# An attention stage whose scores, row transposes, sign bits and sums move into one ring of PSUM bank pairs, with a new order of the work

## The chip, the cores and the metric

The kernel runs on one core of a Trainium2 chip. The metric is the device time of one execution in microseconds (us). TensorE is called PE, VectorE DVE, ScalarE ACT, GpSimd POOL, and SyncE, which issues all the DMAs, SP. PSUM, the memory that PE writes its results to, has eight banks of 512 float32 values in each of 128 partitions.

## The reference

Attention with a hash mask, then two MLP stages on its output; about 18% of the time before is attention, and only attention is changed.

```python
q_bits = (q @ proj > 0)                  # 6 sign bits per query, the same for k
mask   = bucket(q_bits)[:, None] == bucket(k_bits)[None, :]
scores = where(mask, (q @ k.T) / 8, -1e9)
attn   = exp(scores - scores.max(-1))
attn   = attn / (attn.sum(-1) + 1e-9)
x      = attn @ v                        # 2 x 8 heads, 768 tokens, 64 per head
x      = moe(x); out = moe2(x)
```

## The kernel before

There are 16 heads. The queries of a head are worked on in two halves of 384, which makes 32 units; the code calls a unit `u`. Two units (one half of two neighbouring heads) make a pair `n`, and there are 16 pairs. For each unit:

- `s_mm(u, t)`, three times: PE multiplies 128 queries by all 768 keys into the PSUM tile `ps` (lines 376 to 380, two matmuls of together 768 columns), and `s_max(u, t)` reduces it on DVE to the negated maximum of each query (line 383). The mask is part of the product: 12 rows that hold the sign bits stand under the 64 rows of the head.
- `rows_mm(u)` transposes the three columns of maxima on PE (line 392; for the first four units line 390), `rows_cp(u)` copies them on DVE (line 403), and from unit 4 on `rows_move(u)` sends them by DMA into row 96 of the queries' operand.
- `st_mm(u, c)`, six times: the transposed scores of 128 keys, with the row of maxima added, by two matmuls of 384 columns into `pst` (lines 411 and 412); `st_exp(u, c)` takes their exponential on ACT (line 417). `pst` has two banks, so the third `st_mm` waits for the first exponential, and so on.
- `add` sums the exponentials of a unit on POOL (line 429). For a pair, `sum_mm(n)` sums these over the partitions into `psum` (line 455), and `av_mm(n, g)`, twice, multiplies the exponentials by v into `pav` (line 439, twelve matmul passes). `norm` divides, in seven parts on DVE, ACT and POOL with four DMAs (`norm_move`).
- `bits_mm(h)` and `bits_cmp(h)` make the sign bits of a later head (lines 350 and 353); `prep_hi`, `prep_lo`, six `prep_move` and four `bits_move` per head bring operands into place, the moves as DMAs on SP.

Beside this, eight half blocks of weights of the next stage are decoded (`decode`, `weight_hi`, `weight_lo`).

The PSUM of attention before: one tile `s_all` of 1536 values, three banks, holds two score tiles of 768 next to each other, so that the middle bank holds the end of the first and the start of the second. `t_all` is two banks for `pst`; from unit 4 on the row transposes lie in the unused last 128 columns of these. Two banks are `pav`, and the eighth, `ps_m`, is used in turn by the sign bits, the sums and the first units' rows.

The order of the work is made by a planner when the kernel is built: every task has engines, a cost, a due time and the tasks it comes after. Each step takes the task whose planned start plus DELTA times its due time is least. OFF holds a number for each kind of task that is added to its due time. AVD is an offset in the due time of `av_mm`, DUE0 and PACE set the due times of the weight decode. A task with `ring="m"` waits in the plan until the ring's last user is freed. On the chip each engine runs its own list in order, with semaphores between engines.

Of the kernel before, what the change touches and what calls it, by code (L numbers as in the profile page):

```python
# [16 lines left out]
P = 128  # L17
# [5 lines left out]
E = 8  # L23
# [14 lines left out]
NS = 4  # L38
# [4 lines left out]
AVD = 9  # L43
# [7 lines left out]
OFF = {'norm5': 36.2, 'bits_move': 7.5, 'norm1': 2.8, 'bits_mm': 1.0, 'load_v': 17.1, 'norm3': 0.4, 'norm_move': -5.2, 'norm7': 18.8, 'norm0': 8.2, 'weight_load': 32.5, 'weight_lo': 7.6, 'prep_hi': 4.6, 'av_one': -0.2, 'prep_lo': 3.5, 'decode': -2.5, 'norm6': 3.8, 'weight_hi': 23.9, 'rows_mm': 2.9, 'av_mm': -0.5, 'load_qk': -6.3, 'norm4': 13.6, 'rows_cp': -3.6, 'prep_move': 2.8, 'sum_mm': -8.7, 's_max': 2.5, 'rows_move': -4.1, 'bits_cmp': 0.7, 'st_exp': -4.0, 'add': 0.0, 'st_mm': -0.1, 's_mm': -0.3}  # L51
DELTA = 0.0206
RECEIPT = 1.6
DIRECT = 4
DUE0 = 60
PACE = 25
# [15 lines left out]
def lsh_attention_moe_kernel(  # L72
# [111 lines left out]
    def attention():  # L184
        with ExitStack() as a:
# [37 lines left out]
            s_all = ps_s.tile([P, 2 * S], F32, name="ps")  # L223
            t_all = [ps_t.tile([P, 512], F32, name=f"pst{i}") for i in range(2)]
# [60 lines left out]
            def warm_up():  # L285
                warm.append(t_all[0])
                for _ in range(WARM):
                    nc.tensor.matmul(warm[0], xh[:, 0, 0:P], xh[:, 0, 0:512], start=True, stop=True)

            def keep_warm(n):  # L290
                if nm(av_one, 1, 0) in ends:
                    return
                if nm(st_mm, 0, 0) in ends and len(warm) == 1:
                    if nm(av_one, 0, 0) in ends:
                        return
                    warm.append(slot(ps_a, "a", 1, 2, [P, 512], F32, "warm"))
                for _ in range(n):
                    nc.tensor.matmul(warm[-1][:, :FILL], xh[:, 0, 0:P], xh[:, 0, 0:FILL], start=True, stop=True)
# [73 lines left out]
            def s_of(u, t):  # L372
                x = (3 * u + t) % 2
                return s_all[:, x * S:(x + 1) * S]

            def s_mm(u, t):
                s, q0, x = head(u) % NS, half_of(u) * HALF + t * P, (3 * u + t) % 2
                cuts = sorted({0, (512, 256)[x], S} | ({HALF} if u == 0 else set()))
                for a, b in zip(cuts, cuts[1:]):
                    nc.tensor.matmul(s_of(u, t)[:, a:b], sq[s][0:96, q0:q0 + P], bk[s][0:96, a:b], start=True, stop=True)  # L380

            def s_max(u, t):
                nc.vector.tensor_reduce(out=mx_t[u % 2][:, t:t + 1], in_=s_of(u, t), axis=AX.X, op=ALU.max, negate=True)  # L383
# [107 lines left out]
            def task(engines, due, f, *args, after=(), cost=None, lag=0.01, ring=None, frees=None):  # L491
# [14 lines left out]
                    clear=0.6, prep_lo=1.0, add=1.08, norm=1.0, decode=1.3, weight_lo=1.27,  # L506
# [4 lines left out]
            SEEN = {"E": 0.2, "A": 0.05, "D": 0.05, "P": 0.06}  # L511
# [28 lines left out]
            for h in range(NH):  # L540
# [14 lines left out]
                for i in range(2):  # L555
                    task("PD" if h else "D", due - 14.0 + 1 if h else -50, prep_lo, h, i, after=[his[i if h == 0 else 0], *moved] + [los[0]] * i)
                task("E", due - 10.0 if h else -50, bits_mm, h, cost=None if h else 1.1, after=[nm(load_qk, h), nm(proj_parts)], ring="m",
                     frees=nm(bits_cmp, h) if h else nm(bits_cmp, 0, 1, 0))
# [17 lines left out]
            for u in range(NU):  # L576
                h, half, n = head(u), half_of(u), pair_of(u)
                due = 6 * u - 16.0
                for t in range(3):
                    before = nm(s_max, u, 0) if t == 2 else nm(s_max, u - 1, 1 + t)  # L580
                    task("E", due + 2 * t, s_mm, u, t,
                         after=[nm(prep_move, h, 0), nm(prep_move, h, 1), *([nm(bits_move, h, x) for x in range(4)] if h else [nm(bits_cmp, 0, *x) for x in ((0, 1), (1, 1), (half, 0))])] + ([before] if u or t == 2 else []))
                    task("D", due + 2 * t + 0.5, s_max, u, t, after=[nm(s_mm, u, t)] + [nm(rows_mm, u - 2)] * (t == 0 and u > 1))
                direct = u < DIRECT
                task("E", due + 5.5, rows_mm, u, cost=0.14 if direct else None, after=[nm(s_max, u, t) for t in range(3)] + [nm(load_const, 2)] + [nm(warm_up)] * (u == 0), ring="m" if 0 < u < DIRECT else None, frees=nm(rows_cp, u))
# [17 lines left out]
            for n in range(NU // 2):  # L603
# [3 lines left out]
                room = [nm(norm, n - 2, 5)] if n > 1 else []  # L607
# [6 lines left out]
                task("E", due + 8, sum_mm, n, after=[nm(add, u, g, 1) for u in us for g in range(2)], ring="m", frees=nm(norm, n, 0))  # L614
# [716 lines left out]
```

## Time and profile before

| | us |
|---|---|
| three runs | 1551.10, 1552.38, 1553.12 (median 1552.38) |
| the profiled execution | 1549.82 |
| its span, first to last instruction | 1547.90 |
| first instruction to the last matmul of attention | 278.5 |
| PE busy over the span | 1505.7 (97%) |

The profiled execution is 0.17% below the median of the runs; it took 1.92 us more than its span. In the profile a matmul's row gives its start and a duration that runs on while the next one starts, since matmuls are pipelined: what one costs PE's stream is the distance to the next start. "[0.34 <-DVE mx L383]" behind a row means that the engine stood idle for 0.34 us and that DVE's instruction of line 383 ended that. "x2" counts instructions that are shown in one row.

### The profile page before, as it was taken

The page shows a single profiled execution, that of the slowest core. Times are in us where ns is not written, and L with a number is a line of the kernel's source. Part 1 is how long each engine was busy: PE and PEld are TensorE (multiplying, and loading weights), DVE is VectorE, ACT ScalarE, POOL GpSimd, SP SyncE. Part 2 cuts the span into 40 slices and gives each one's busy share as a digit, 9 for nine tenths or more (in the row PEclk, how much of TensorE's full clock was granted, in tenths as well). Part 3 has the DMA queues.
Part 4 walks back from the last instruction along what each step waited for, and adds up shares of the span by engine and source line. Part 5 has one row for each costly group of instructions (what it writes and reads, how often), then busy time and mean ns, then how long its engine had stood idle before and what let it go on. Part 6 is the DMA issues. An engine that isn't in the chain of part 4 may idle for free.

```text
span 1547.9 us, 20241 instructions
## 1 busy us (share of the span) xinstructions
PE 1505.7 (97%) x7454; PEld 1256.1 (81%) x7454; DVE 861.9 (56%) x1400; ACT 628.7 (41%) x1113; POOL 902.1 (58%) x750
## 2 busy tenths in 40 slices
PE   8888888999999999999999999999999999999998
PEld 5454444688888789898989898989898999999997
DVE  6666666777752666666443467654535344445353
ACT  4444444555432443334333333343333333333331
POOL 5556666543332476666666666667666666666661
PEclk9999999999999999999999999999999999999999
DMA  7356451222110012222222221213222222221211
GB/s 185 113 123 149 109 129 42 82 83 82 64 59 1 28 56 81 69 68 69 68 67 70 67 68 66 69 60 116 64 70 66 69 68 68 68 69 68 69 55 41
DMA packets 69561, 116.80 MB, mean 75 GB/s; under 512 B 21348, under 2 KB 23512, under 8 KB 69464
## 3 DMA queue, kind: packets, MB, share of 16 engines
q1 hardware_dynamic: 69464, 115.53, 24.8%
q8 instruction: 58, 0.95, 0.3%
q14 instruction: 39, 0.32, 0.1%
HBM read 93.41 MB, written 3.15 MB: 62 GB/s over the span
## 4 chain that ended last, share of the span: by engine, by line
PE 91%; DVE 5%; DMA 1%; ACT 1%; issue 1%; SPq 1%; DVEq 0%; ACTq 0%
PE y L1183 34%; PE u L1116 30%; PE y L819 8%; PE pav L439 4%; DVE mx L383 4%; PE ps L380 3%; PE h L796 3%; PE h L794 3%; PE h L795 3%; PE pst L411 1%; PE psum L455 1%; PE pst L412 1%; DMA other<-own 1%; ACT p L417 0%; PE lg L847 0%
## 5 line engine op out<-in xcount | busy, mean ns | idle before, releaser
L1124 ACT ACTIVATE gh<-c 128x384 fp32r<-128x384 f32 x256 | 134.6, 526 | 174.3 <-DVE c L1136 172.3
L1129 DVE SCALAR_TENSOR_TENSOR gl<-c,gh 128x384 fp32r<-128x384 f32 x256 | 195.6, 826 | 0.0
L1136 DVE TENSOR_TENSOR u<-u,p 128x384 f32<-128x384 f32 x64 | 35.7, 558 | 284.2 <-PE u L1116 282.4
L1183 PE MATMUL y<-ww,gh 128*128 128x512 f32 x768 | 186.6, 391 | 0.0
L1183 PE MATMUL y<-w,gh 128*128 128x512 f32 x768 | 186.0, 391 | 0.0
L1183 PEld LDWEIGHTS y<-w,gh 128*128 128x128 f32 x768 | 143.7, 188 | 28.9
L1183 PEld LDWEIGHTS y<-ww,gh 128*128 128x128 f32 x768 | 143.7, 188 | 28.8
L417 ACT ACTIVATE p<-pst 128x384 f32<-128x384 f32 x192 | 86.0, 489 | 118.5 <-PE pst L412 77.0
L999 POOL TENSOR_TENSOR w<-stage,w 128x1024 fp32r<-128x1024 f32 x32 | 76.6, 2393 | 89.1 <-ACT w L995 89.1
L999 POOL TENSOR_TENSOR ww<-stage,ww 128x1024 fp32r<-128x1024 f32 x32 | 76.5, 2391 | 81.6 <-ACT ww L995 81.6
L383 DVE TENSOR_REDUCE mx<-ps 128x1 f32<-128x768 f32 x96 | 90.6, 953 | 47.2 <-PE ps L380 46.9
L819 PE MATMUL y<-gh,w 128*128 128x512 f32 x336 | 109.8, 389 | 0.0
L158 POOL TENSOR_TENSOR stage<-stage,sgn 128x512 f32<-128x512 f32 x32 | 43.3, 1354 | 104.7 <-DVE sgn L156 90.4
L429 POOL TENSOR_TENSOR pa<-p,p 128x384 f32<-128x384 f32 x64 | 66.1, 1033 | 61.6 <-ACT p L417 61.6
L1183 PE MATMUL y<-ww,gl 128*128 128x512 f32 x384 | 98.2, 389 | 0.0
L1183 PE MATMUL y<-w,gl 128*128 128x512 f32 x384 | 97.6, 389 | 0.0
L995 ACT CAST ww<-stage 128x1024 fp32r<-128x1024 f32 x32 | 33.6, 1050 | 157.5 <-PE y L1183 157.5
L975 POOL TENSOR_TENSOR wa<-stage,wa 128x512 fp32r<-128x512 f32 x32 | 45.5, 1421 | 88.8 <-ACT wa L970 79.7
L995 ACT CAST w<-stage 128x1024 fp32r<-128x1024 f32 x32 | 33.6, 1049 | 154.5 <-PE y L1183 154.5
L975 POOL TENSOR_TENSOR wx<-stage,wx 128x512 fp32r<-128x512 f32 x32 | 45.4, 1419 | 80.4 <-ACT wx L970 80.4
L1116 PE MATMUL u<-tw,w 128*128 128x384 f32 x480 | 91.8, 336 | 0.0
L1116 PE MATMUL u<-tw,ws 128*128 128x384 f32 x480 | 91.6, 336 | 0.0
(204 smaller groups left out, 3634.3 us busy)
## 6 DMA issues: line engine op xcount, KB each, us to landing
stage<-in_w_dram SPq DMA_DIRECT2D x160, 512.0 KB
raw<-in_qk_dram SPq DMA_DIRECT2D x13, 384.0 KB
sb<-hi SPq DMA_DIRECT2D x20, 192.0 KB
vt<-in_v_dram SPq DMA_DIRECT2D x16, 192.0 KB
out_dram<-acc SPq DMA_DIRECT2D x11, 256.0 KB
wx<-hi SPq DMA_DIRECT2D x14, 192.0 KB
zq<-hi SPq DMA_DIRECT2D x10, 192.0 KB
ak<-hi SPq DMA_DIRECT2D x10, 192.0 KB
```

The lines of the kernel that those rows point to most:

```text
L383: nc.vector.tensor_reduce(out=mx_t[u % 2][:, t:t + 1], in_=s_of(u, t), axis=AX.X, op=ALU.max, negate=True)
L417: nc.scalar.activation(p_t[u, c][:, :HALF], st_t.pop((u, c))[:, :HALF], AF.Exp, scale=0.125)
L429: (nc.gpsimd if e == "P" else nc.vector).tensor_add(t, (t if x else p_t[u, 3 * g])[:, :HALF], p_t[u, 3 * g + 1 + x][:, :HALF])
L439: nc.tensor.matmul(av_t[n][64 * e:64 * e + 64, :WIDE], vt[head(u) // 2 % 2][:, c, e, :], p_t[u, c][:, :WIDE], start=(c == 0), stop=(c == N ...
L819: nc.tensor.matmul(yps[j], x, y, start=(head and m == 0), stop=(tail and m == 2))
L975: nc.gpsimd.tensor_sub(a[:, 1, 0:512], t[:, 0, :], f32(a)[:, 0, 0:512])
L995: nc.scalar.copy(wbuf[u % 2]["w"][:, 0, :], staged["u", u, 1].rearrange("p c n -> p (c n)"))
L999: nc.gpsimd.tensor_sub(y[:, 1, :], t, f32(y)[:, 0, :])
L1116: nc.tensor.matmul(bank[x], weight(u, a, m, kc), moving(u, b, mm, kc), start=(first and n == 0), stop=(n == 5), skip_group_check=not first)
L1124: nc.scalar.activation(hi, src, AF.Relu)
L1129: nc.vector.scalar_tensor_tensor(out=lo, in0=src, scalar=0.0, in1=f32(hid_u[u, c][0]), op0=ALU.max, op1=ALU.subtract)
L1183: nc.tensor.matmul(y_t[t], (hi, hi, lo)[m][:, t % 3 * P:(t % 3 + 1) * P], y, start=(k == 0 and first), stop=(k == NF // 2 - 1 and last),)
```

## The change

Score tiles, row transposes, sign bits and sums are now all taken from one ring, `next_r`, of two slots; a slot is two whole banks, [128, 2, 512]. A score tile uses 384 columns of each of its two banks, by two matmuls of 384 columns. `s_all` and `ps_m` are gone; the four banks of the ring take their place. `pst` keeps its two banks but no longer holds row transposes. In the plan a task of ring "r" waits for the last but one user to be freed. Head 0's bits are made in a bank of `pav`. The constants of the planner are new: all 31 numbers of OFF (`st_mm` from -0.1 to 2.1, `s_mm` from -0.3 to 2.4, `sum_mm` from -8.7 to -0.6, ...), DELTA, AVD, DUE0, PACE and two costs. No arithmetic is changed.

```diff
-AVD = 9
+AVD = 6
...
-DELTA = 0.0206
+DELTA = 0.0524
...
-DUE0 = 60
-PACE = 25
+DUE0 = 20
+PACE = 24
...
-            ps_s = a.enter_context(tc.tile_pool(name="ps_s", bufs=1, space=bass.MemoryType.PSUM))
+            ps_r = a.enter_context(tc.tile_pool(name="ps_r", bufs=1, space=bass.MemoryType.PSUM))
...
-            ps_m = a.enter_context(tc.tile_pool(name="ps_m", bufs=1, space=bass.MemoryType.PSUM))
...
-            s_all = ps_s.tile([P, 2 * S], F32, name="ps")
-            t_all = [ps_t.tile([P, 512], F32, name=f"pst{i}") for i in range(2)]
+            used_r = [0]
...
-            def next_m(name):
-                return slot(ps_m, "m", 0, 1, [P, 512], F32, name)
+            def next_r(name):
+                used_r[0] += 1
+                return slot(ps_r, "r", used_r[0], 2, [P, 2, 512], F32, name)
...
-                psb_t[h] = next_m("pbits")
+                psb_t[h] = next_r("pbits")[:, 0] if h else slot(ps_a, "a", 1, 2, [P, 512], F32, "pbits")
...
-            def s_of(u, t):
-                x = (3 * u + t) % 2
-                return s_all[:, x * S:(x + 1) * S]
-
             def s_mm(u, t):
-                s, q0, x = head(u) % NS, half_of(u) * HALF + t * P, (3 * u + t) % 2
-                cuts = sorted({0, (512, 256)[x], S} | ({HALF} if u == 0 else set()))
-                for a, b in zip(cuts, cuts[1:]):
-                    nc.tensor.matmul(s_of(u, t)[:, a:b], sq[s][0:96, q0:q0 + P], bk[s][0:96, a:b], start=True, stop=True)
+                s, q0 = head(u) % NS, half_of(u) * HALF + t * P
+                s_t[u, t] = next_r("ps")
+                for j in range(2):
+                    nc.tensor.matmul(
+                        s_t[u, t][:, j, :HALF], sq[s][0:96, q0:q0 + P], bk[s][0:96, j * HALF:(j + 1) * HALF], start=True, stop=True
+                    )
...
-                m = t_all[u % 2][:, HALF:] if u >= DIRECT else next_m("prow") if u else t_all[1]
+                m = next_r("prow")[:, 0]
...
-                t = t_all[c % 2]
+                t = slot(ps_t, "t", NKC * u + c, 2, [P, 512], F32, "pst")
...
-                sum_t[n] = next_m("psum")
+                sum_t[n] = next_r("psum")[:, 0]
...
-            SEEN = {"E": 0.2, "A": 0.05, "D": 0.05, "P": 0.06}
+            SEEN = {"E": 0.28, "A": 0.05, "D": 0.05, "P": 0.06}
...
                     use = ring_use.setdefault(t[7], [])
-                    if use:
-                        if use[-1] not in ends:
+                    if len(use) >= 2:
+                        if use[-2] not in ends:
                             return None
-                        r = max(r, ends[use[-1]])
+                        r = max(r, ends[use[-2]])
```

What the new plan does to PE's list is seen in the middle of attention, around one pair's sums. Before, all that is not a score or an `st_mm` stands in one block: a row transpose, the first `av_mm`, the sums, another row transpose, and then the second `av_mm` and a later head's sign bits:

```order
L392 MATMUL pst_160<-idt,mx_157 3x128
L439 MATMUL pav<-p_144,vt_128 64x386
L439 MATMUL pav<-p_136,vt_128 64x386
L439 MATMUL pav<-p_145,vt_128 64x386
L439 MATMUL pav<-p_137,vt_128 64x386
L439 MATMUL pav<-p_146,vt_128 64x386
L439 MATMUL pav<-p_138,vt_128 64x386
L455 MATMUL psum<-pa_150,ones 32x384
L455 MATMUL psum<-pa_151,ones 32x384
L455 MATMUL psum<-pa_152,ones 32x384
L455 MATMUL psum<-pa_153,ones 32x384
L392 MATMUL pst_159<-idt,mx_156 3x128
```

In the changed kernel the six `st_mm` of one unit, with two to four score tiles, stand between the two `av_mm` of a pair. The list around the sums (line numbers are three to seven lower there):

```order
L452 MATMUL psum<-pa_147,ones 32x384
L452 MATMUL psum<-pa_148,ones 32x384
L452 MATMUL psum<-pa_149,ones 32x384
L452 MATMUL psum<-pa_150,ones 32x384
L347 MATMUL pbits<-raw,pf 32x192 x4
L436 MATMUL pav<-p_138,vt_125 64x386
L436 MATMUL pav<-p_144,vt_125 64x386
L436 MATMUL pav<-p_139,vt_125 64x386
L436 MATMUL pav<-p_145,vt_125 64x386
L436 MATMUL pav<-p_140,vt_125 64x386
L436 MATMUL pav<-p_146,vt_125 64x386
L389 MATMUL prow<-idt,mx_153 3x128
```

One `av_mm` with the sums and the bits is a block, the other `av_mm` with a row transpose another, and before and behind each stand `st_mm` and scores.

The second place is where PE writes scores. Before, two neighbouring score tiles are written into the one tile `ps_158` (names with their numbers here):

```order
L380 MATMUL ps_158<-sb1_118 128x256
L380 MATMUL ps_158<-sb1_118 128x512
L411 MATMUL pst0_159<-zq3_123,ak3_126 128x384
L412 MATMUL pst0_159<-sb3_120 128x384
L380 MATMUL ps_158<-sb1_118 128x512
L380 MATMUL ps_158<-sb1_118 128x256
```

and in the changed kernel every user of the ring is a tile of its own, here a row transpose and two score tiles:

```order
L389 MATMUL prow_1344<-idt_69,mx1_154 3x128
L408 MATMUL pst_1346<-zq2_119,ak2_122 128x384
L409 MATMUL pst_1346<-sb2_116 128x384
L373 MATMUL ps_1354<-wx0_78 128x384 x2
L408 MATMUL pst_1360<-zq2_119,ak2_122 128x384
L409 MATMUL pst_1360<-sb2_116 128x384
L373 MATMUL ps_1365<-wx0_78 128x384 x2
```

The third place is DVE's list behind a pair's sums in the changed kernel: each row that reads `ps`, `psum`, `pbits` or `prow` frees a slot of the ring, and other work stands among them.

```order
L378 TENSOR_REDUCE mx0_153<-ps_1533 128x1
L465 STREAM_TRANSPOSE rs_127<-psum_1549 128x384
L350 TENSOR_SCALAR bit_1569<-pbits_1556,cst_71 128x192
L156 TENSOR_SCALAR sgn1_87<-stage_794 128x512
L420 TENSOR_TENSOR xl_75<-xu_126,xh_74 128x384
L400 TENSOR_SCALAR row_1584<-prow_1577 3x128
L378 TENSOR_REDUCE mx1_154<-ps_1586 128x1
```

Before, `psum`, `pbits` and `prow` are not in the scores' banks, so that of these rows only the two reductions free what the scores wait for.

## Rows read from the trace of the kernel before

**Rows 1.** Windows: us, then busy (instructions) of PE, PEld, DVE, ACT, POOL; PEclk, DMA share, GB/s.
```profile
156.50:188.10 31.60, 27.72 (x158) 15.39 (x160) 20.91 (x34) 13.59 (x30) 20.50 (x20) 1.00 0.48 118
251.70:278.50 26.80, 25.27 (x143) 12.14 (x142) 16.68 (x30) 13.77 (x30) 18.64 (x18) 1.00 0.07 21
300.00:340.00 40.00, 40.00 (x178) 33.10 (x178) 31.65 (x43) 25.37 (x42) 17.02 (x10) 1.00 0.28 90
```

**Rows 2.** Timeline, PE and DVE, 120 to 124 us: start, us, engine, instruction, [idle before].
```profile
120.46 0.61 PE L380 MATMUL ps<-sb 96*128 96x256 f32 x2 [0.36 <-DVE mx L383]
121.11 0.96 DVE L383 TENSOR_REDUCE mx<-ps 128x1 f32<-128x768 f32 x1 [0.37 <-PE ps L380]
...
122.12 0.62 PE L380 MATMUL ps<-sb 96*128 96x512 f32 x2 [0.34 <-DVE mx L383]
122.78 0.96 DVE L383 TENSOR_REDUCE mx<-ps 128x1 f32<-128x768 f32 x1 [0.23 <-PE ps L380]
```

**Rows 3.** Timeline, PE and then DVE, 96 to 99 us.
```profile
96.27 0.51 PE L380 MATMUL ps<-sb 96*128 96x512 f32 x2
96.62 0.34 PE L411 MATMUL pst<-zq,ak 128*128 128x384 f32 x1
96.80 0.34 PE L412 MATMUL pst<-sb 97*128 97x384 f32 x1
...
98.69 0.61 PE L380 MATMUL ps<-sb 96*128 96x256 f32 x2 [1.01 <-DVE mx L383]
...
96.82 1.82 DVE L383 TENSOR_REDUCE mx<-ps 128x1 f32<-128x768 f32 x2 [0.73 <-PE ps L380]
```

**Rows 4.** Timeline, PE, one block of av, sums, rows and bits.
```profile
124.25 0.27 PE L392 MATMUL pst<-idt,mx 128*3 128x128 f32 x1
124.45 2.17 PE L439 MATMUL pav<-p,vt 128*64 128x386 f32 x12
126.54 0.85 PE L455 MATMUL psum<-pa,ones 128*32 128x384 f32 x8
127.33 0.27 PE L392 MATMUL pst<-idt,mx 128*3 128x128 f32 x1
127.53 2.17 PE L439 MATMUL pav<-p,vt 128*64 128x386 f32 x12
129.62 0.53 PE L350 MATMUL pbits<-raw,pf 128*32 128x192 f32 x8
130.09 0.45 PE L411 MATMUL pst<-zq,ak 128*128 128x384 f32 x1
```

**Rows 5.** Timeline, PE, where no scores are left.
```profile
270.25 0.44 PE L411 MATMUL pst<-zq,ak 128*128 128x384 f32 x1 [0.27 <-ACT p L417]
...
271.52 0.44 PE L411 MATMUL pst<-zq,ak 128*128 128x384 f32 x1 [0.26 <-ACT p L417]
```

**Rows 6.** Timeline, SP: the first of each kind of DMA issue, 156 to 174 us.
```profile
156.83 0.72 SPq L332 DMA_DIRECT2D sb<-row  x1
157.60 1.61 SPq L332 DMA_DIRECT2D sb<-bit  x2
160.41 2.48 SPq L459 DMA_DIRECT2D other<-own  x4
...
163.88 1.15 SPq L332 DMA_DIRECT2D sb<-hi  x2
...
165.84 0.47 SPq L259 DMA_DIRECT2D raw<-in_qk_dram  x1
...
173.91 1.31 SPq L265 DMA_DIRECT2D vt<-in_v_dram  x2
```

**Rows 7.** Timeline, ACT, start of attention.
```profile
24.48 0.87 ACT L417 ACTIVATE p<-pst 128x384 f32<-128x384 f32 x2 [0.33 <-PE pst L412]
34.85 0.87 ACT L417 ACTIVATE p<-pst 128x384 f32<-128x384 f32 x2 [9.50 <-PE pst L412]
```

**Rows 8.** Windows, columns as in rows 1: the stretch with a lower clock.
```profile
104.00:108.00 4.00, 3.87 (x13) 2.46 (x15) 2.33 (x5) 1.21 (x3) 1.01 (x1) 0.54 0.28 60
```

More of the change, by code (lines that the diff above doesn't have):

```diff
@@ L50 @@
 AHEAD = (1, 2)
-OFF = {'norm5': 36.2, 'bits_move': 7.5, 'norm1': 2.8, 'bits_mm': 1.0, 'load_v': 17.1, 'norm3': 0.4, 'norm_move': -5.2, 'norm7': 18.8, 'norm0': 8.2, 'weight_load': 32.5, 'weight_lo': 7.6, 'prep_hi': 4.6, 'av_one': -0.2, 'prep_lo': 3.5, 'decode': -2.5, 'norm6': 3.8, 'weight_hi': 23.9, 'rows_mm': 2.9, 'av_mm': -0.5, 'load_qk': -6.3, 'norm4': 13.6, 'rows_cp': -3.6, 'prep_move': 2.8, 'sum_mm': -8.7, 's_max': 2.5, 'rows_move': -4.1, 'bits_cmp': 0.7, 'st_exp': -4.0, 'add': 0.0, 'st_mm': -0.1, 's_mm': -0.3}
-DELTA = 0.0206
+OFF = {'weight_lo': 16.9, 'add': -3.4, 'weight_load': -20.3, 'norm6': 66.2, 'prep_hi': -4.2, 'norm_move': -19.9, 'load_qk': 0.9, 'norm0': -16.1, 'load_v': -23.6, 'decode': 9.4, 'bits_mm': -6.9, 'norm1': -61.2, 'norm5': 11.9, 'st_exp': -7.0, 'norm7': 23.6, 'rows_cp': -10.6, 'av_mm': 0.7, 'rows_move': -20.0, 'rows_mm': 3.0, 'norm4': -35.4, 'norm3': 9.3, 'sum_mm': -0.6, 'bits_cmp': -14.6, 'av_one': 3.6, 'weight_hi': 63.6, 's_max': 0.0, 'st_mm': 2.1, 'prep_move': 6.5, 'prep_lo': -0.4, 'bits_move': -5.8, 's_mm': 2.4}
+DELTA = 0.0524
 RECEIPT = 1.6
 DIRECT = 4
-DUE0 = 60
-PACE = 25
+DUE0 = 20
+PACE = 24
 NX = 1
@@ L285, in warm_up @@
             def warm_up():
-                warm.append(t_all[0])
+                warm.append(slot(ps_t, "t", 0, 2, [P, 512], F32, "warm"))
                 for _ in range(WARM):
@@ L290, in keep_warm @@
             def keep_warm(n):
-                if nm(av_one, 1, 0) in ends:
+                if nm(av_one, 0, 0) in ends:
                     return
                 if nm(st_mm, 0, 0) in ends and len(warm) == 1:
-                    if nm(av_one, 0, 0) in ends:
-                        return
-                    warm.append(slot(ps_a, "a", 1, 2, [P, 512], F32, "warm"))
+                    warm.append(slot(ps_a, "a", 0, 2, [P, 512], F32, "warm"))
                 for _ in range(n):
@@ L505, in attention @@
                 "P": dict(
-                    clear=0.6, prep_lo=1.0, add=1.08, norm=1.0, decode=1.3, weight_lo=1.27,
+                    clear=0.6, prep_lo=1.0, add=1.03, norm=1.0, decode=1.3, weight_lo=1.27,
                 ),
@@ L556, in attention @@
                     task("PD" if h else "D", due - 14.0 + 1 if h else -50, prep_lo, h, i, after=[his[i if h == 0 else 0], *moved] + [los[0]] * i)
-                task("E", due - 10.0 if h else -50, bits_mm, h, cost=None if h else 1.1, after=[nm(load_qk, h), nm(proj_parts)], ring="m",
-                     frees=nm(bits_cmp, h) if h else nm(bits_cmp, 0, 1, 0))
+                task("E", due - 10.0 if h else -50, bits_mm, h, cost=None if h else 1.1, after=[nm(load_qk, h), nm(proj_parts)] + [nm(bits_move, h - 2, x) for x in range(4) if h > 2], ring="r" if h else None, frees=nm(bits_cmp, h))
                 if h:
@@ L579, in attention @@
                 for t in range(3):
-                    before = nm(s_max, u, 0) if t == 2 else nm(s_max, u - 1, 1 + t)
                     task("E", due + 2 * t, s_mm, u, t,
-                         after=[nm(prep_move, h, 0), nm(prep_move, h, 1), *([nm(bits_move, h, x) for x in range(4)] if h else [nm(bits_cmp, 0, *x) for x in ((0, 1), (1, 1), (half, 0))])] + ([before] if u or t == 2 else []))
+                         after=[nm(rows_mm, u - 2)] * (t == 0 and u > 1) + [nm(prep_move, h, 0), nm(prep_move, h, 1), *([nm(bits_move, h, x) for x in range(4)] if h else [nm(bits_cmp, 0, *x) for x in ((0, 1), (1, 1), (half, 0))])], ring="r", frees=nm(s_max, u, t))
                     task("D", due + 2 * t + 0.5, s_max, u, t, after=[nm(s_mm, u, t)] + [nm(rows_mm, u - 2)] * (t == 0 and u > 1))
                 direct = u < DIRECT
-                task("E", due + 5.5, rows_mm, u, cost=0.14 if direct else None, after=[nm(s_max, u, t) for t in range(3)] + [nm(load_const, 2)] + [nm(warm_up)] * (u == 0), ring="m" if 0 < u < DIRECT else None, frees=nm(rows_cp, u))
+                task("E", due + 5.5, rows_mm, u, cost=0.14 if direct else None, after=[nm(s_max, u, t) for t in range(3)] + [nm(load_const, 2)] + [nm(warm_up)] * (u == 0), ring="r", frees=nm(rows_cp, u))
                 task("D", due + 6, rows_cp, u, cost=0.5 if direct else None, after=[nm(rows_mm, u)] + [nm(rows_move, u - 1)] * (u - 1 >= DIRECT))
@@ L606, in attention @@
                 due = 6 * us[1]
-                room = [nm(norm, n - 2, 5)] if n > 1 else []
+                room = [nm(norm, n - 2, 5)] if n > 1 else [nm(bits_cmp, 0, 1, 0)] * n
                 for g in range(NKC // AVG):
@@ L613, in attention @@
                              + [nm(load_v, head(u)) for u in part] + [nm(clear_slots, j) for j in range(2)] * (n < 2))
-                task("E", due + 8, sum_mm, n, after=[nm(add, u, g, 1) for u in us for g in range(2)], ring="m", frees=nm(norm, n, 0))
+                task("E", due + 8, sum_mm, n, after=[nm(add, u, g, 1) for u in us for g in range(2)] + [nm(norm, n - 2, 5)] * (n > 1), ring="r", frees=nm(norm, n, 0))
                 raw = [nm(bits_mm, x) for x in (1, 2)] + [nm(prep_lo, x, i) for x in (1, 2) for i in range(2)]
```

4 lines of the change are left out of this document (3 added, 1 removed).

## The prediction

> **What bounds the kernel now.** I read the page's slices first, to find where PE is not full, then windows of attention, then PE's and DVE's timelines side by side. Behind attention PE has no gap (last row of [rows 1]), and the change touches nothing there, so only the first 278.5 us count. In them PE runs through a regular pattern: two pairs take 31.6 us, of which the profile shows PE busy for 27.72 [rows 1].
>
> The reader is to see in [rows 2] what PE waits for. A score tile is written at 120.46, its reduction runs from 121.11 to 122.07, the next tile is written at 122.12, and so on: each tile starts 0.05 us after the reduction of the tile just before it, though there are two places for tiles. One tile each 1.66 us, then, of which the reduction is 0.96. There is an exception that tells the mechanism: at 96.27 a tile is written without a wait, before the reduction of the earlier one has started (it comes at 96.82, two in a row), and the one after that, at 98.69, waits for the end of both [rows 3]. So a write waits for those reductions of the neighbouring tile that stand ahead of it in the program. What the two tiles have in common is the middle bank.
>
> The other half of the pattern is the block of av, sums, rows and bits. From 124.25 to 130.09 it takes 5.84 us of PE's stream without a gap [rows 4], and no score is written in it. Together: two pairs have 12 score tiles and two blocks, 12 x 1.66 + 2 x 5.84 = 31.6 us, just what the window has [rows 1]. Score chain and block follow each other; that is the bound, 15.8 us a pair.
>
> **What the change does to one pair.** *Removed: the wait for the neighbour.* Each ring slot has its own two banks, so the next tile waits for the last but one user. PE's own work for a pair, from starts to starts: 12 `st_mm` of two matmuls at 0.18 each, 4.3 us (96.62 to 96.80, [rows 3]); 6 score tiles at 0.35, 2.1 us (96.27 to 96.62, [rows 3]); the block 5.84 [rows 4]. Sum 12.2.
>
> *Where that wait goes.* Next in line is the pair of `pst` banks: without any score, two `st_mm` follow the two before by 1.27 us [rows 5], because an exponential must free the bank, and PE needs only 0.7 of it. So six `st_mm` of a unit take at least 2 x 1.27 + 0.7 = 3.25 us. Two or three score tiles fit into the two gaps of 0.55 and the end; with four (every second unit in the new order) I take 3.7. A pair: 3.25 + 3.7 + 5.84 = 12.8, and 0.3 for being cut into two blocks instead of one (the start behind a block costs 0.28 between two matmuls against 0.18, and a row transpose 0.2, [rows 4]): 13.1 us. This is the lower bound.
>
> *Moved: the av products.* AVD 9 to 6 and the new offsets put one `av_mm` behind each unit. This costs PE nothing but the 0.3, and gives DVE its reductions in two halves of a pair. The last exponential of a pair has to wait until the second `av_mm` has freed its buffer, perhaps 0.1 us a pair.
>
> *Other engines.* Per pair DVE is busy 10.5 us, POOL 10.3 and ACT 6.8 (the first window over two, [rows 1]). POOL gets six more subtractions or additions in attention by the new order, about 0.4 us a pair. All stay under 13.1, but no longer by much, and each runs in order: ACT's 0.8 us conversion of a head now stands between exponentials. SP comes closest. Per pair it issues 2 rows at 0.72, 4 bits at 0.81, 6 moves at 0.58, 4 `norm_move` at 0.62, one head's v at 0.65, one raw load at 0.47, and a weight load every second pair, which I count as 0.25: 12.0 us [rows 6]. With 0.05 between issues (156.83 + 0.72 to 157.60, [rows 6]), 18.5 issues make 13.0. SP hence would have nothing to spare at 13.1, and it also waits for results in order. For its friction I bound the pair between 13.1 (none) and 14.9, where a pair pays two full DMA waits more (0.9 us each, as a bare `st_mm` gap plus a late row; an estimate from the largest idle in [rows 3], 1.01). I take 13.8 to 13.9, nearer to the lower end, as the SP list holds these moves a unit or more ahead of their use.
>
> *Start and end.* In the first 60 us exponentials stop for 9.5 us [rows 7] while av products and scores alternate; the new list keeps `st_mm` going there. A pair of that stretch gains about 2 us more than a regular one, and the stretch at the lower clock (granted 0.54, mostly the 1.2 GHz level, after PE had stood waiting for scores; [rows 8]) costs before some 2 us that a denser PE need not pay. I take 4 for both, between 0 and 7. The first `st_mm` comes a score or two sooner, since unit 0's rows no longer stand behind unit 1's scores: 1.5 us, one tile of [rows 2]. The last two pairs have nearly no scores left and take 26.8 us [rows 1]; no gain there. The weight decode is due earlier and done well before the end in both; the next stage's first short waits remain. DVE's reduction over two banks has the same 768 values: nothing.
>
> **Sum.** 14 pairs x (15.8 - 13.85 = 1.95) = 27.3, and 4, and 1.5: 33 us less. Against the profiled execution's own 1549.8 that is 1517 us. (That execution lies 2.6 below the median of the runs shown.)
>
> **Rivals.** *SP becomes the bound.* For it: 12.0 us of issues per pair, and DVE's list waits for `norm_move` ahead of the next reductions, so a late SP holds scores as well. Against: SP has idle stretches before, as from 159.2 to 160.4 [rows 6], and heads are prepared more than ten us ahead. At 14.9 a pair the gain is 14 x 0.9 + 3 = 16 us: 1534. The Trainium skill, DMA: Bandwidth & Descriptors, section Issuing engines are not separate DMA queues, says that the time a sequencer takes to start a DMA is usually small next to the DMA itself; by that rule SP would not bind and the pair would be 13.1, 1506 us in all. The rows speak against the rule in this kernel, with many small moves.
>
> *Slower: the shared ring.* Before, sums, bits and rows had places of their own; now 10 users per pair (6 scores, 2 rows, one sum, one bits) go in turn through two slots, each freed by DVE, whose list holds long work between them. A sum that waits for POOL, or a late transposition of it, stops scores, and behind these in PE's list `st_mm` and av. PE gives back all of the 2.7 us between 13.1 and 15.8 when the mean wait per user reaches 0.27 us. With 0.34 each, as PE stands idle per tile in [rows 2], the pair is 13.1 + 3.4 = 16.5: 14 x 0.7 - 4 = 6 us more, 1556. Against it: a slot's last but one user was in most places of the list read at least one `st_mm` and one score earlier, 1 us, and the sums stand in front of a 2.1 us `av_mm` that hides their transposition.
>
> *The wait stays.* If the order between tiles came from the reduction itself and not from the shared bank, tiles would still follow each other at 1.66, six a pair, and at best overlap with av: 1540 to 1552, say 1548. The exception in [rows 3] speaks against it, but no row before has two tiles without a common bank. The Trainium skill, PSUM — Partial Sum Buffer, section PSUM bank collisions raise a hardware error, says that PE's writes and DVE's reads must be kept apart by bank and not by address; by that rule the wait in [rows 2] is the bank's, and goes.
>
> **How the numbers follow.** Forecast (pair of 13.1 to 14.4, start term 0 to 7): 0.66, 1502 to 1526. SP binds: 0.19, 1526 to 1541. Wait stays: 0.06. Shared ring, slower: 0.07. Something else: 0.02. The range 1502 to 1536 holds nearly all of the first and two thirds of the second, 0.79. A measurement of this kernel can tell 0.2% or 3 us from no change: faster by more than that 0.89 (forecast, SP, and half of the stayed wait with half of the rest), same 0.03, slower 0.08.
>
> **What would show it.** Attention's last sum ends near 245 instead of 278. In the timeline a score tile starts while the reduction before it still runs, and PE's idle time in front of scores by DVE, before in nearly every tile, mostly vanishes; idle in front of `st_mm` by ACT grows to some 1 us a pair. Pairs repeat in 13.8 us. If SP binds, its issues stand without idle and reductions come behind `nr`. If the ring binds, scores, sums or rows on PE wait for DVE with over 0.27 each. The forecast is wrong if pairs still take 15 us or more, or if the next stage gets slower.

## The result, and the profile after

The changed kernel takes 1506.14 us (median of four runs, 1504.71 to 1506.72), the kernel before 1552.75 in the same comparison (1551.10 to 1553.62). The ratio is 0.970, with a 95% interval of 0.9683 to 0.9716: faster by 46.6 us, where 1517 was forecast, in the range 1502 to 1536. The profiled execution after took 1506.02 us with a span of 1504.2, 43.7 less than the span before.

The page's part 1 of the changed kernel (busy us, share of the span and instructions of each engine), then the head of the chain that ended last (the chain of work followed back from the last instruction, as shares of the span), then the groups of exponentials and of score reductions (line, engine, operation, busy us, mean ns, idle time before them):

```profile
PE 1487.8 (99%) x7448; PEld 1254.2 (83%) x7448; DVE 866.2 (58%) x1394; ACT 628.9 (42%) x1113; POOL 910.8 (61%) x756
...
PE 93%; DVE 2%; DMA 2%; SPq 1%; issue 1%; ACT 0%; POOL 0%; DVEq 0%; ACTq 0%
...
L414 ACT ACTIVATE p<-pst 128x384 f32<-128x384 f32 x192 | 88.4, 490 | 79.1 <-PE pst L409 73.0
...
L378 DVE TENSOR_REDUCE mx<-ps 128x1 f32<-128x768 f32 x96 | 88.4, 946 | 11.4 <-PE ps L373 10.9
```

In the kernel before the head of that chain was

```profile
PE 91%; DVE 5%; DMA 1%; ACT 1%; issue 1%; SPq 1%; DVEq 0%; ACTq 0%
```

so DVE's share of it falls from 5 to 2%. PE's share of the span rises from 97 to 99%. Of the 43.7 us, 26 were idle time of PE and 18 busy time, though its matmuls are nearly as many (7454 before, 7448 after): a row lasts longer at a lower clock and where it starts after a wait (a score tile 0.61 us in [rows 2], 0.51 without a wait in [rows 3]). Where PE stood, its waits show, here from 60 to 260 us (who waited, for whom, us in total, times, longest; some 12 pairs before and 13 after, whose attention ends at 235 us). First the kernel before:

```profile
PE ps L380 <- DVE mx L383: 22.3, 52, 1.2
PE pst L411 <- ACT p L417: 2.0, 10, 0.3
```

and of the changed kernel:

```profile
PE pbits L347 <- DMA raw<-in_qk_dram: 3.3, 4, 1.4
...
PE pst L408 <- ACT p L414: 1.0, 3, 0.6
PE ps L373 <- DVE mx L378: 0.8, 3, 0.3
...
PE pbits L347 <- DVE mx L378: 0.7, 1, 0.7
PE prow L389 <- DVE mx L378: 0.7, 2, 0.4
```

Scores waited 52 times for the reduction of their neighbour, and now wait three times for a reduction. How it looks in the stream, from the changed kernel's timeline, PE's rows and then DVE's (start, us, engine, instruction):

```profile
148.78 0.51 PE L373 MATMUL ps<-sb 96*128 96x384 f32 x2
149.13 0.34 PE L408 MATMUL pst<-zq,ak 128*128 128x384 f32 x1
149.31 0.34 PE L409 MATMUL pst<-sb 97*128 97x384 f32 x1
149.48 0.51 PE L373 MATMUL ps<-sb 96*128 96x384 f32 x2
149.83 0.34 PE L408 MATMUL pst<-zq,ak 128*128 128x384 f32 x1
150.01 0.34 PE L409 MATMUL pst<-sb 97*128 97x384 f32 x1
150.28 0.44 PE L408 MATMUL pst<-zq,ak 128*128 128x384 f32 x1
150.56 0.34 PE L409 MATMUL pst<-sb 97*128 97x384 f32 x1
150.74 0.52 PE L373 MATMUL ps<-sb 96*128 96x384 f32 x2
...
149.33 2.92 DVE L378 TENSOR_REDUCE mx<-ps 128x1 f32<-128x768 f32 x3 [0.42 <-PE ps L373]
```

Set beside [rows 2]: there a tile started 0.05 us after the end of the reduction before it, one tile each 1.66 us. Here the tile of 149.48 is written while the reduction of the tile of 148.78 runs (149.33 to 150.30), and the three reductions stand one right behind the other. The third tile, 150.74, has to wait for that first reduction alone, which ended 0.4 us earlier.

Windows (us, then busy time of PE, PEld, DVE, ACT, POOL; granted clock, DMA share, GB/s) over eight pairs in the middle, from the start of the 49th `st_mm` to that of the 145th. First the kernel before:

```profile
85.53:216.82 131.29, 113.97 (x627) 63.96 (x627) 85.52 (x142) 60.33 (x129) 80.08 (x79) 0.97 0.52 126
```

then the changed kernel, with the stretch of [rows 8] behind it:

```profile
71.28:181.10 109.82, 105.67 (x636) 62.96 (x636) 92.78 (x146) 61.71 (x133) 89.14 (x84) 1.00 0.62 155
...
104.00:108.00 4.00, 3.88 (x30) 1.82 (x27) 3.54 (x5) 1.26 (x4) 3.53 (x4) 1.00 0.52 138
```

Eight pairs took 131.3 us and take 109.8, 16.41 and 13.73 us a pair. The granted clock, 0.54 in that stretch before, is 1.00 in all of them after: the fall to the 1.2 GHz level is gone along with the waits that stood before it. The kernel before has a second such stretch, at 0.50 from 12.1 to 19.0 us, where its first `st_mm` starts; the changed kernel has none.

Where the time came from is seen by counting `st_mm` in the timeline (192 in each kernel; starts of the first matmul of each, us):

| | 1st | 49th | 145th | 192nd | last sum |
|---|---|---|---|---|---|
| before | 16.85 | 85.53 | 216.82 | 273.24 | 277.76 |
| after | 13.63 | 71.28 | 181.10 | 230.33 | 234.87 |
| won in the stretch | 3.2 | 11.0 | 21.5 | 7.2 | 0.0 |

Together 42.9 us in attention. The first matmul of the next stage follows at 236.50 instead of 278.54, now after a wait of 0.8 us for DVE. This stage is 1.7 us shorter; it has one wait less at its start, 1.4 us for a weight from ACT. 42.0 and 1.7 make the 43.7 of the span.

### The profile page after: what moved, and what is told of

The parts are those of the page before. It is cut to its first block, busy times and chain, and to the rows that moved or that the text cites. A ratio compares the mean times of both kernels' runs of the same rounds, so it can differ in the third digit from the quotient of the medians.

```text
span 1504.2 us, 20253 instructions
## 1 busy us (share of the span) xinstructions
PE 1487.8 (99%) x7448; PEld 1254.2 (83%) x7448; DVE 866.2 (58%) x1394; ACT 628.9 (42%) x1113; POOL 910.8 (61%) x756
## 4 chain that ended last, share of the span: by engine, by line
PE 93%; DVE 2%; DMA 2%; SPq 1%; issue 1%; ACT 0%; POOL 0%; DVEq 0%; ACTq 0%
PE y L1178 35%; PE u L1111 31%; PE y L814 9%; PE pav L436 4%; PE h L791 3%; PE h L790 3%; PE h L789 3%; PE pst L408 2%; PE ps L373 2%; PE pst L409 1%; DMA raw<-in_qk_dram 1%; DVE mx L378 1%; PE psum L452 1%; SPq L329 1%; PE pbits L347 0%
## 5 line engine op out<-in xcount | busy, mean ns | idle before, releaser
L970 POOL TENSOR_TENSOR wx<-stage,wx 128x512 fp32r<-128x512 f32 x32 | 45.4, 1419 | 80.5 <-ACT wx L965 80.5
L1178 PEld LDWEIGHTS y<-w,gl 128*128 128x128 f32 x384 | 72.0, 188 | 15.5 <-DVE gl L1124 0.6
```

Of the source, the lines that this page charges most:

```text
L970: nc.gpsimd.tensor_sub(a[:, 1, 0:512], t[:, 0, :], f32(a)[:, 0, 0:512])
L1178: nc.tensor.matmul(y_t[t], (hi, hi, lo)[m][:, t % 3 * P:(t % 3 + 1) * P], y, start=(k == 0 and first), stop=(k == NF // 2 - 1 and last),)
```

## The experiments

Twelve kernels were run. The "before" of each comparison had a median of 1550.8 to 1552.2 us. The last five columns are counted as in the table above, in the one execution of each kernel that was profiled; "pair" is the distance from the 49th to the 145th `st_mm` over eight. For e8 that execution was the longest of six, 1565.3 us, 6.4 above the median; for the others it lies within 1.3 us of the median.

| kernel | us | ratio to before (95%) | 1st | 49th | 145th | 192nd | pair |
|---|---|---|---|---|---|---|---|
| e1: ring, old plan | 1516.98 | 0.978 (0.975 to 0.981) | 16.19 | 75.90 | 185.60 | 241.74 | 13.71 |
| e2: new plan, old banks | 1548.49 | 0.998 (0.996 to 0.999) | 17.90 | 90.31 | 210.29 | 268.22 | 15.00 |
| e5: ring in one tile | 1563.51 | 1.008 (1.005 to 1.011) | 18.26 | 98.98 | 232.87 | 286.77 | 16.74 |
| e6: norm copies on ACT | 1511.81 | 0.975 (0.972 to 0.977) | 13.62 | 73.78 | 186.45 | 236.76 | 14.08 |
| e7: after, more on SP | 1540.06 | 0.993 (0.991 to 0.995) | 13.17 | 78.59 | 205.68 | 261.49 | 15.89 |
| e8: before, more on SP | 1558.91 | 1.005 (1.003 to 1.006) | 17.02 | 87.11 | 227.88 | 284.29 | 17.60 |
| e9: after, more on PE | 1521.74 | 0.981 (0.979 to 0.984) | 13.63 | 76.67 | 194.18 | 246.72 | 14.69 |
| e10: before, more on PE | 1558.99 | 1.005 (1.003 to 1.007) | 16.96 | 88.93 | 222.01 | 281.37 | 16.64 |
| e11: loads due sooner | 1517.68 | 0.979 (0.976 to 0.982) | 13.63 | 75.11 | 190.70 | 243.27 | 14.45 |
| e12: sums added on PE | 1513.42 | 0.975 (0.974 to 0.977) | 13.68 | 73.63 | 189.34 | 239.12 | 14.46 |

e3 and e4 stand apart, below.

**Which part of the change does it: the ring or the plan?** e1 is the changed kernel with the planner's constants of before, e2 the kernel before with the new constants.

```diff
# e1, from the changed kernel
-AVD = 6
+AVD = 9
-OFF = {'weight_lo': 16.9, 'add': -3.4, ...
+OFF = {'norm5': 36.2, 'bits_move': 7.5, ...
-DELTA = 0.0524
+DELTA = 0.0206
-DUE0 = 20
-PACE = 24
+DUE0 = 60
+PACE = 25
```

> The ring of bank pairs alone: OFF, DELTA, AVD, DUE0, PACE and the two planner costs are those of before. If the gain comes from the wait at the shared bank, tiles no longer follow the reduction of the neighbour, a pair goes from 15.8 to about 14 us and the kernel takes 1510 to 1530 us. If the new order is what gains, the ring alone stays at 1540 us or more.

> The planner's constants of the change alone, with the PSUM layout of before. If the shared bank is the cause, score tiles still follow each other at 1.66 us; the two av blocks can lie beside one reduction each, so a pair takes 14.5 to 15.8 us: 1530 to 1550 us. If the order is what gains: 1510 or less.

With the ring alone the pair is 13.71 us, as with both (13.73): the ring is enough for all that a regular pair wins, and the plan, with AVD 9 or 6, makes no difference to it. Both times lie in the ranges for the ring as the cause. The ring alone wins 35.2 us by the medians, the plan alone 3.7, both 46.6, so the two are worth more together. The table shows where: the ring with the old plan starts its first `st_mm` at 16.19, 2.6 later than the changed kernel, loses another 2.1 up to the 49th, and needs 56.1 us for the last 47 (before 56.4, changed kernel 49.2). One place is a gap of 1.57 us that ends at 196.91, where an `st_mm` waits for the DMA of its row. From there on the granted clock is at the lower level for 7 us, which costs at most the 3.4 us that are missing from 8 us at 0.57 (columns as above):

```profile
196.00:204.00 8.00, 6.26 (x24) 3.58 (x26) 7.34 (x13) 2.47 (x5) 4.39 (x4) 0.57 0.36 90
```

The new plan is thus worth what it saves at the two ends, once the scores no longer hold PE; of the 6.9 us at the end up to half is the clock behind that one wait. On the old banks it spreads the scores over more of the pair, which falls to 15.00, but the chain stays, and the start and the end give half of that back (72.4 us from the 1st to the 49th against 68.7, 57.9 for the last 47 against 56.4). Another 4.4 us are lost in the next stage, which starts 6.9 us sooner: PE waits 2.8 us there for the weight from ACT (1.4 before), and the granted clock is at 0.50 from 284.3 to 291.1. e2's largest wait of PE from 60 to 260 us:

```profile
PE ps L380 <- DVE mx L383: 17.7, 31, 1.2
```

**Is it the bank that the write waited for, or the tile?** e5 is the changed kernel with the two slots as the halves of one tile of four banks. No two users share a bank, but all share a tile.

```diff
+            r_all = ps_r.tile([P, 2, 2, 512], F32, name="ring4")
...
-                return slot(ps_r, "r", used_r[0], 2, [P, 2, 512], F32, name)
+                return r_all[:, used_r[0] % 2]
```

> The changed kernel with its two slots as the two halves of one tile of four banks, nothing else. If what a reader waits for goes by the bank (the theory), the time is that of the changed kernel, 1506 us, within 5 us of it, and PE waits for DVE's reductions in less than 5 us of the attention. If it goes by the tile (the rival), PE waits for each reduction again and the time is 1540 to 1552 us.

1563.5 us: slower than the kernel before. Its timeline, PE and then DVE:

```profile
118.03 0.62 PE L374 MATMUL ring<-sb 96*128 96x384 f32 x2 [0.35 <-DVE mx L379]
...
119.70 0.53 PE L348 MATMUL ring<-raw,pf 128*32 128x192 f32 x8 [0.35 <-DVE mx L379]
...
118.69 0.96 DVE L379 TENSOR_REDUCE mx<-ring 128x1 f32<-128x768 f32 x1 [0.71 <-PE ring L374]
```

The sign bits of 119.70 go into the other half, two banks that nobody reads, and yet start 0.05 us after the end of the reduction (118.69 + 0.96 = 119.65), with 0.35 us of idle time before them. The wait comes with the common tile, the one thing in which e5 differs from the changed kernel: in this program the semaphores order a write behind the read of another part of the same PSUM tile, though the two touch different banks. So the middle bank of before, to which the prediction put the wait, is not needed for it; `s_all` was one tile too. Whether a common bank between two tiles would also hold the write was not tried. And with all ten users of a pair in one such tile the ring is no better than the old layout (pair 16.74 against 16.41, at a granted clock of 0.95 against 0.97 in that stretch, so part of the difference is the clock); the time lies above the 1540 to 1552 us of the rival too.

**What sets the pace now? SP?** The first attempt issued each `norm_move` twice, in the changed kernel (e3) and in the kernel before (e4):

```diff
                 nc.sync.dma_start(out=other[32 * x:32 * x + 32], in_=own[32 * y:32 * y + 32])
+                nc.sync.dma_start(out=other[32 * x:32 * x + 32], in_=own[32 * y:32 * y + 32])
```

> The changed kernel with each of the four norm_move DMAs of a pair issued twice (the same copy, so the result is unchanged): 4 x 0.62 us and their gaps more on SP per pair. If SP's issues bind the pair now (24.9 to 26.6 us of issues in 27.7 us for two pairs), some 12 pairs lengthen by 2 to 2.7 us: 1528 to 1540 us. If PE and the exponentials bind, less than 8 us more: below 1514.

> The same doubling in the kernel before, where SP has 3 us of each pair free. By the theory that scores bind there and SP does not: 0 to 10 us more than before, 1552 to 1563. If SP was a bound already: 25 us more or above, 1577.

Both missed by some 80 to 110 us: 1641.0 (ratio 1.058) and 1640.9 us (1.058). SP's timeline of e3, and behind it its largest wait from 60 to 260 us, show why:

```profile
105.49 0.56 SPq L456 DMA_DIRECT2D other<-own  x1
109.31 0.54 SPq L457 DMA_DIRECT2D other<-own  x1
```

```profile
SPq L457 <- DMA other<-own: 66.1, 36, 4.6
```

The second copy writes what the first one writes, so SP waits until the first has landed, 1.8 us each on the mean, with all other moves queued behind it. This measures a blocked queue and not the price of an issue. With SP's queue held up like this the layout of PSUM is worth nothing: both kernels then take the same time.

e7 and e8 do it cleanly, with four more copies per pair into a tile `spare` that nothing reads:

```diff
+            spare = out_p.tile([P, HALF // 32], F32, name="spare")
...
                 nc.sync.dma_start(out=other[32 * x:32 * x + 32], in_=own[32 * y:32 * y + 32])
+                nc.sync.dma_start(out=spare[32 * x:32 * x + 32], in_=own[32 * y:32 * y + 32])
```

> The changed kernel with four more copies per pair on SP's queue, each to memory that nothing reads and that no other copy writes. By the theory that SP has almost no slack left in the changed kernel, 2.5 to 2.7 us more per pair in some 12 pairs, 1530 to 1540 us. By the rival, that PE's own work sets the pace, under 1514 us.

> The kernel before with the same four copies more per pair. By the theory that the scores' chain binds there and SP has 2 to 3 us of slack per pair, 1552 to 1563 us. If SP sets the pace in the kernel before too, 1577 us or more.

The changed kernel gets 33.9 us slower (1540.06 against 1506.14), the kernel before 8.1 (1558.91 against 1550.79 in the same comparison): at the upper end of the range for an SP that is nearly full after, and inside the one for an SP with slack before. Windows of e7, two pairs each from the 49th `st_mm` on, say how much of it is SP (columns as before):

```profile
78.59:109.81 31.22, 27.45 (x169) 15.87 (x168) 24.10 (x38) 16.70 (x36) 24.34 (x24) 1.00 0.57 137
109.81:140.94 31.13, 26.35 (x160) 15.67 (x158) 23.87 (x37) 14.60 (x32) 20.78 (x20) 1.00 0.53 137
140.94:174.53 33.59, 28.67 (x160) 16.49 (x158) 22.25 (x37) 15.51 (x34) 22.55 (x22) 0.90 0.54 128
```

At the full clock a pair takes 15.6 us, 1.9 more than in the changed kernel, of the added 4 x 0.60 us of issues and 0.05 us behind each, 2.6 us: SP has some 0.7 us a pair to spare. SP's own rows say the same. From the 49th to the 145th `st_mm` its 148 issues sum to 96.7 us of 109.8 (88%) in the changed kernel; with 0.05 us behind each that leaves 5.7 us, 0.7 a pair. Before, 148 issues take 98.3 us of 131.3 (75%). The third window of e7 is 2.4 us longer at a granted clock of 0.90. In it PE stood 3.94 us for a load, until 149.2 us, and from 148.0 us on the clock was at the lower level, 0.50 and 0.64 of full in the two stretches of 4 us from there. The trace of e7 has four such stretches between 66 and 285 us, so its 33.9 us are not SP's issues alone. The profiled execution of e8 has them too. By its span it is 15.2 us longer than the kernel before; 6.1 of these stand in the two pairs from the 49th `st_mm`, 41.4 us at a clock of 0.79 where the kernel before took 35.4 at 0.90, and 4.1 in the next stage, which the copies do not touch. PE's waits of e7 show where it hurts:

```profile
PE pbits L348 <- DMA raw<-in_qk_dram: 20.7, 9, 3.9
PE pst L410 <- DMA sb<-row: 2.1, 3, 0.9
```

The load of a head's q and k comes late, and the sign bits wait for it, at the head of PE's list.

The opposite, e6, takes the four copies off SP and issues them from ACT's queue:

```diff
-                nc.sync.dma_start(out=other[32 * x:32 * x + 32], in_=own[32 * y:32 * y + 32])
+                nc.scalar.dma_start(out=other[32 * x:32 * x + 32], in_=own[32 * y:32 * y + 32])
```

> The changed kernel with the copies of the row of norms issued from ACT's queue instead of SP's, which takes some 2.5 us of issues off SP per pair. If SP's queue now sets the pace of the pairs (its issues sum to 25 to 26.6 us in 27.7 us), 1490 to 1500 us; if PE and the exponentials set it, 1503 to 1512 us, since ACT has idle time for the issues.

1511.8 us, 5.7 slower than the changed kernel. The time lies in the range for a pace that SP does not set: SP's issues fall to 66% of the stretch, and nothing is won. In the 200 us from 60 on PE now waits 2.6 us for exponentials (1.0 in the changed kernel), among which ACT's issues stand, and 4.7 us for the loads of q and k (3.3), though SP has more room.

**PE?** e9 and e10 issue the first matmul of every `st_mm` twice, 12 x 0.18 = 2.16 us of PE's stream per pair:

```diff
-                nc.tensor.matmul(t[:, :HALF], ak[s][:, k], zq[s][:, q], start=True, stop=False)
+                nc.tensor.matmul(t[:, :HALF], ak[s][:, k], zq[s][:, q], start=True, stop=True)
+                nc.tensor.matmul(t[:, :HALF], ak[s][:, k], zq[s][:, q], start=True, stop=False)
```

> The changed kernel with the first matmul of every st_mm issued twice, 12 matmuls of 0.18 us a pair, 2.2 us. If PE's own stream sets the pace of the pairs now (the theory), all of it shows in nearly 16 pairs: 1535 to 1542 us. If PE still has room and another engine sets the pace, under 1515 us.

> The kernel before with the same doubled matmul. In its chain of scores a tile takes 1.66 us, of which PE fills 0.35 and up to two st_mm of 0.36; a doubled matmul in each fits as well. By the theory 1550 to 1562 us. If PE had no room there, 1575 us or more.

The changed kernel takes 15.6 us more, between what the theory and the rival gave, so neither holds as it was put: 0.96 of 2.16 us a pair show. The window of e9 from the 49th to the 145th `st_mm`:

```profile
76.67:194.18 117.51, 116.61 (x733) 80.35 (x732) 93.83 (x144) 64.26 (x133) 88.41 (x83) 1.00 0.58 145
```

There PE's rows are full, 116.6 of 117.5 us. Its pair of 14.69 us less the added 2.16 is 12.5 us: PE's own work in the changed kernel, or less if these rows hide waits, which leaves it some 1.2 us of room in 13.73. In the kernel before 8.0 us show of the same addition, as expected; the gaps of the score chain take most of it. So in the changed kernel neither PE (12.5) nor SP (some 0.7 us short of full) is the one bound: the pace of 13.73 lies just above both. That each runs its own list in order and holds the other up now and then fits this, but no run shows it by itself.

**Can it be had faster?** e11 moves the loads of q and k 4.9 sooner in the plan, against the 3.3 us that PE waits for them; e12 forms the total of the sums on PE, so that the copy to `own`, the four `norm_move` and an addition fall away.

```diff
# e11
-OFF = {..., 'load_qk': 0.9, ...}
+OFF = {..., 'load_qk': -4, ...}
# e12; the planner's tasks for what falls away go too
-                for u in members(n):
-                    for x in range(2):
-                        r = 64 * (head(u) % 2) + 32 * x
-                        nc.tensor.matmul(sum_t[n][r:r + 32, :HALF], ones[:, 0:32], pa_t[u, x], start=True, stop=True)
+                for x in range(2):
+                    for u in members(n):
+                        r = 64 * (head(u) % 2)
+                        nc.tensor.matmul(sum_t[n][r:r + 64, :HALF], ones[:, 0:64], pa_t[u, x], start=x == 0, stop=x == 1)
...
-                    nc.vector.scalar_tensor_tensor(out=nr, in0=other, scalar=EPS, in1=own, op0=ALU.add, op1=ALU.add)
+                    nc.vector.tensor_scalar(out=nr, in0=first, scalar1=EPS, scalar2=None, op0=ALU.add)
```

> The changed kernel with the due time of the loads of q and k moved 4.9 sooner, against the 3.3 us that PE stands before sign bits for them. If these waits are on the path and the rest of the order stays as good, 1500 to 1504 us; if SP's other moves come later for it, 1505 to 1515 us.

> The changed kernel with the total of the sums formed on PE: each of its sums is written to 64 partitions and the second added onto the first in PSUM, so the copy to own, the four copies to other on SP's queue and the addition fall away. PE pays 8 matmuls at 0.175 us (as av's, 12 in 2.1 us) instead of 0.78 us, 0.6 us a pair, of which by the run with doubled matmuls a bit under half shows, 4 to 5 us in all. SP saves 2.5 us of issues a pair. If SP's queue is the nearest bound of the changed kernel (the runs with more copies showed nearly all of them), the sum is a gain, 1485 to 1502 us. If relieving SP gives nothing, as with the copies moved to ACT, 1508 to 1518 us.

1517.7 and 1513.4 us: neither beats the changed kernel. e11 came out above both ranges, e12 in the one for "relieving SP gives nothing". In e11 the planner moves many of SP's other issues when the loads move, and PE's waits from 60 to 260 us grow instead, one of them to 5.3 us:

```profile
PE pbits L347 <- DMA raw<-in_qk_dram: 7.4, 2, 5.3
PE pst L408 <- ACT p L414: 2.5, 7, 1.3
PE pst L409 <- DMA sb<-row: 2.0, 1, 2.0
```

The windows of e11, two pairs each from the 49th `st_mm` on, put what it loses between the 49th and the 145th in one place:

```profile
75.11:103.40 28.29, 28.20 (x170) 16.50 (x170) 23.24 (x35) 15.89 (x34) 24.15 (x23) 1.00 0.55 131
103.40:128.50 25.10, 24.75 (x146) 15.10 (x146) 20.27 (x33) 12.97 (x30) 18.59 (x19) 1.00 0.64 148
128.50:163.62 35.12, 29.65 (x168) 17.75 (x168) 24.06 (x37) 17.24 (x37) 25.67 (x25) 0.90 0.64 138
163.62:190.70 27.08, 26.38 (x160) 15.50 (x158) 23.61 (x37) 14.37 (x32) 22.89 (x22) 1.00 0.64 158
```

Six pairs take 80.5 us, 13.4 each and no slower than in the changed kernel; the two with the long wait and a clock of 0.90 behind it take 35.1. Another 3.8 us are lost before the 49th `st_mm` and 3.3 behind the 145th. Whether an order with the loads sooner and without these losses is faster was not tried.

In e12 SP's issues are down to 69% of the stretch, PE's waits are small (2.0 us for exponentials, 1.2 for reductions, 1.1 for a load), and the pair is 14.46. PE pays for it: the row of a pair's sums lasts 1.46 us instead of 0.85. Twice, then, SP was relieved and the time did not fall. Both relieving edits also put work elsewhere (ACT's issues, PE's wider sums), and e12's plan is a new one, so what holds the pair at 13.7 when SP has room stays open. No version here is faster than the changed kernel.

## Why the prediction was right, and where it was off

*The bound.* Right: the chain of scores and reductions. Its wait went from 22.3 us in the 200 us shown to 0.8, and the ring without the new plan gives the whole gain of a regular pair (e1). The cause behind the wait was put to the wrong thing: "What the two tiles have in common is the middle bank" holds, but they also had the tile in common, and e5 shows that this is enough. The change gives each user banks and a tile of its own, so the forecast of the time did not suffer; that was luck. A ring with banks of its own inside one tile would have turned it from a gain of 46 into a loss of 13 us.

*The pair after.* Forecast 13.85, measured 13.73 over the eight pairs in the middle. PE's own work was put at 12.2 and 0.3 for the cut into two blocks; e9 gives 12.5 or less. SP's issues were put at 18.5 a pair and 13.0 us with the gaps; the rows have 148 in eight pairs and the same 13.0. The friction of 0.75 above 13.1 was laid to SP. e7 and SP's rows bear out that SP is nearly full, e6 and e12 that it is not alone.

*The sum.* It was 33 us and should have been 43 (43.7 between the profiled executions; 46.6 by the medians, since the execution from which the forecast counts lies below its median); the steps that were mis-sized, by the counts of `st_mm`:

| stretch | forecast | measured |
|---|---|---|
| first `st_mm` | 1.5 | 3.2 |
| pairs 1 to 4 (4 x 1.95, 2 of the start term) | 9.8 | 11.0 |
| pairs 5, 6, with the lower clock (2 x 1.95, 2 of the term) | 5.9 | 6.8 |
| pairs 7 to 12 (6 x 1.95) | 11.7 | 14.7 |
| pairs 13 to 16 (2 x 1.95, none in the last two) | 3.9 | 7.2 |

The largest error is the gain per pair, 1.95. From the 73rd to the 145th `st_mm` (120.91 to 216.82 before, 99.90 to 181.10 after) it is 15.99 - 13.53 = 2.45 us: the 15.8 of before, read from a single window of two pairs, was 0.2 low, and 13.85 was 0.3 high. The other is the end: "no gain there" for the last two pairs, but 1.5 us were won in them and 5.7 in the two before. The ring with the old plan (e1) does not have these 7.2, wins only 0.3 there, so they hang on the plan, to which the prediction gave no term at all beyond the start; up to 3.4 of them are the lower clock behind a late row in e1. The first `st_mm` was put at one tile: in the new list three score tiles stand ahead of unit 0's rows instead of five, and before PE waited 1.14 and 1.05 us for reductions in front of the last two of these. The clock in the middle was sized about right, as far as it can be told apart: before, the two pairs with the stretch at 0.54 took 35.4 us, 3.4 more than two others, and 1.9 of the 6.8 us won in them go beyond the gain of two regular pairs.

*The signs to look for.* The last sum was forecast near 245 and came at 234.87. Scores over a running reduction: seen. "Idle in front of `st_mm` by ACT grows to some 1 us a pair": not seen, 1.0 us in 200; yet e9 finds 1.2 us a pair of room on PE. Some 0.5 us a pair is idle time that the rows show (109.82 less 105.67 us in eight pairs), mostly before sign bits. The rest stands under no name, and rows of matmuls that get longer are where part of it can be. At 150.28 above, the first matmul of an `st_mm` has 0.44 us and the next starts 0.28 later, where at 149.13 it is 0.34 and 0.18, with no idle time named at either.

*The rivals.* "SP becomes the bound", at 14.9 a pair: not so at the pace measured, but only some 0.7 us a pair away. The Trainium skill, DMA: Bandwidth & Descriptors, section Issuing engines are not separate DMA queues, led by its rule to 1506 us, which is the time measured; that is luck, for the way there is not the one measured. By that rule SP's issues would not count and the pair would be 13.1; it is 13.73, and 2.6 us more of issues and the gaps behind them cost 1.9 us. The runs decide against the rule for a queue with 18 moves a pair, 0.65 us of issue each on the mean. "Slower: the shared ring", from a mean wait of 0.27 us per user: scores, rows and bits together waited 2.2 us for DVE's reductions from 60 us to the end of attention, with 119 users of the ring, 0.02 each. e5 is that rival come true by another road. "The wait stays": it went. The Trainium skill, PSUM — Partial Sum Buffer, section PSUM bank collisions raise a hardware error, speaks of keeping engines apart by bank; by that alone e5 would have cost nothing, and it takes 57 us more than the changed kernel. The order that the program keeps is coarser than what that section asks for.

## What to carry to other kernels

When a producer and a consumer alternate although there are two places for the data, look for anything that the places share, and give each place a tile of its own, not only banks of its own. Once such a wait is gone, measure how much room the next engines have by adding a known amount of harmless work to each in turn; the part of it that does not show is the room, and idle times in the rows can miss it. The gain per step is to be read over many steps of the trace, not over one window.

## What the runs showed of the hardware

In this program a second copy to the same destination holds SP's whole queue until the first has landed, 1.8 us on the mean and up to 4.6 here (e3), where an issue to another place costs 0.60 us (e7). The lower clock was seen at the end of a single wait of PE: 3.94 us of idle time in e7, with PE busy for 1.22 us from 144 to 148 us, and then a granted clock of 0.50 and 0.64 in the next two stretches of 4 us, though PE was busy for 6.8 of these 8. It does not follow every wait: in the kernel before PE stands for 1.40 and 1.70 us between 286.6 and 290.8 us, and the granted clock stays at 1.00. With more work on PE in the kernel before (e10) the clock does not fall in the middle of attention: the two pairs from the 49th `st_mm` on take 34.5 us at a granted clock of 1.00, against 35.4 at 0.90 without that work. And of 2.16 us a pair of additional matmuls PE took 1.2 without a change of pace, where the trace of the changed kernel names 0.5 us a pair of idle time (e9).
